# Two tiles of batches 0 and 1 through seven half-size products, the weights' differences earlier, and mask products on 120 of 128 columns

## The chip, the cores and the metric

The kernel runs on one core of one Trainium2 chip. The core has a matrix engine (PE; its weight loads are shown as PEld), a vector engine (DVE), an activation engine (ACT), a general engine (POOL), a queue engine for transfers (SP), and 16 DMA engines. Every engine works through its own list of instructions in order, and engines wait for each other by semaphores. The metric is the device time of one execution in microseconds; smaller is better.

## The reference, cut to what matters

```
q, k, v: (4 batches, 8 heads, 768 tokens, 64)
scores = (q @ k^T) / 8
mask   = same or neighbouring block of 32 tokens | first or last block, as row or as column
         | three sampled blocks per block row
attn   = softmax(where(mask, scores, -1e9));   x = attn @ v       -> (4, 768, 512)
a1     = alpha1 * x + beta1
u      = x + lam * (w_tok @ a1)                # over the 768 tokens
a2     = alpha2 * u + beta2
out    = u + lam * (relu(a2 @ w_ch1) @ w_ch2)  # 512 -> 2048 -> 512
```

The change concerns the last product, `relu(...) @ w_ch2` (768 x 2048 by 2048 x 512 in each batch), and the mask of the attention.

## The kernel before, in words

The 768 tokens of a batch are six tiles of 128 (`o` = 0 to 5): partition p of tile o holds token 6p + o. Two heads form a pair, so there are 16 pairs, four to a batch. The scores of a pair are made in nine units: an "A" unit is 2 x 128 keys by four query tiles (512 columns), a "B" unit holds the two remaining query tiles of two key pairs. A unit is `emit_qk` (PE, L600, into PSUM), `emit_exp` (ACT, L618, into the tile eT), from pair 5 on `emit_keep` (DVE, L635: eT times the 0/1 mask `mask01`, all 1024 numbers of a partition), and `emit_pv` or `emit_pv_keys` (PE, L647 or L670, weights times v, with a sum column). When a head is complete `emit_finish` divides (DVE, L687, L688) and `emit_a1pp` scales (two steps, L704 and L705, mostly on POOL).

The rest of a batch's work is cut into jobs: `job_tok2` (L844, the product over tokens; the addition L856 and two casts L863 on DVE), `emit_udma` (a transposing transfer, L894, issued by SP), `emit_uscale` (DVE, L885), `job_f1` (L910, the first channel product, 32 jobs in a batch; ACT writes the relu into `hts`, L917) and, for the second channel product, `job_f2` (L930): a quarter of a tile, four matmuls of 512 columns into one PSUM tile `mm`; the fourth quarter is followed by the addition into `x_sb` (DVE, L939) and the store (SP, L943). `mm` tiles rotate through three PSUM banks.

Batches 2 and 3 (`STR = (2, 3)`) already compute part of the second channel product in another way. Take tiles t and t+3 as two block rows, the hidden units as two halves, and the output columns as two halves (`lo`, `hi`). The eight half-size block products are replaced by seven:

```
weights, once:   T1 = B12 - B11   T2 = B22 - T1   T4 = B21 - T2   T3 = B22 - B12       job_t, DVE, L972
per two tiles:   X1 = A21 + A22   X2 = X1 - A11   A21 <- A11 - A21   A12 <- A12 - X2   job_s 1..4, DVE, L1018
products:        1: A11 B11   2: A12 B21   6: X2 T2   5: X1 T1                         job_p, PE, L1044
                 7: (A21) T3  4: A22 T4    3: (A12) B22
```

Each product is eight matmuls of 256 columns and is followed by an addition into `x_sb` (`plus`, DVE, L1054). Products 1, 6 and 5 accumulate in one PSUM bank, and 7 and 4 in another: the bank is read by the addition behind each of them before the next product is accumulated on top. The T blocks lie in buffers of the first phase that are free by then (`qTs`, `kTs`, `qk0`, `tmore`). In batch 2 these are tiles (1, 4) and (2, 5), in batch 3 all six.

What sets the order: the first 45 units (pairs 0 to 4) follow a plan with due times; all that comes after them follows the strings `W1`, `W2`, `W2L`, `W3`, one string for three units. A letter emits one thing: `q` the three units' score products and the first exponential, `x` an exponential, `k` a mask product, `p` a value product of one key pair, `f` a `job_f1`, `g` the next job of the second channel product, `T` a `job_tok2`, `d` an `emit_udma`, `v` an `emit_uscale`, `Y` a copy of v, `A` a `job_t` of two rows, `S` a `job_s`. On each engine the instructions run in this order. `g` takes its jobs from a list: 24 per batch where all six tiles go by `job_f2`. The strings are named here by their lines: W2 is L55 to L66, W2L L69 to L80. While W2 runs, batch 0's second channel product ends (strings L55 to L59); while W2L runs, batch 1's does (L69 to L73), with the same letters. By the first score product of each string the profile has them at these times: L45 at 63.55 us, L55 at 102.14, L56 at 105.62, L57 at 116.32, L58 at 120.14, L59 at 123.47; and in W2L, L70 at 174.16, L71 at 184.87, L72 at 188.69, L73 at 192.01.

## Time and profile before

| | |
|---|---|
| median of 3 runs | 300.72 us (300.29 to 301.11) |
| profiled execution | 300.64 us |
| its span, first to last instruction | 298.6 us |
| PE busy | 292.3 us (98%) |
| DVE busy | 219.5 us (74%) |
| ACT busy | 218.6 us (73%) |
| POOL busy | 109.7 us (37%) |

The span is 2.04 us shorter than the profiled execution's own time. The busy share of PE is a share of time in which at least one matmul is in flight; it is not a share of the peak.

### The profile page before, as it was taken

The numbers are of one execution on the slowest core, as the hardware profiler recorded it, in microseconds if no ns is written. First come the engines' busy times: TensorE is split into PE (matmuls) and PEld (weight loads), VectorE is DVE, ScalarE is ACT, GpSimd is POOL, SyncE is SP. The second block draws the span as 40 slices with busy tenths as digits, with TensorE's granted clock in tenths as the row PEclk, the third lists the DMA queues.
The fourth block names the chain that finished last, engine by engine and source line by source line (L and its number), as shares of the span: only waits on it lengthen the run. The fifth ranks groups of instructions, "written<-read, shape, count | busy, mean of one in ns | idle before, by whom it ended". The sixth has DMA issues, their size and how long they took to land.

```text
span 298.6 us, 7517 instructions
## 1 busy us (share of the span) xinstructions
PE 292.3 (98%) x3113; PEld 194.5 (65%) x3113; DVE 219.5 (74%) x434; ACT 218.6 (73%) x324; POOL 109.7 (37%) x149
## 2 busy tenths in 40 slices
PE   7999999999999999999999999999999999999995
PEld 3688888665567565565576465565566589666884
DVE  4988999995678797978778777892756889204674
ACT  4999999998799963999779581999869734677100
POOL 8997887632443710355323340344320300000000
PEclk9999999999999999999999999999999999999999
DMA  6999999971392992729844777727321112300032
GB/s 178 201 193 168 192 156 204 190 121 26 94 151 50 120 201 75 121 61 134 119 85 76 121 119 143 114 72 89 50 61 30 25 37 57 113 0 2 0 140 74
DMA packets 57273, 31.08 MB, mean 104 GB/s; under 512 B 37204, under 2 KB 54016, under 8 KB 57240
## 3 DMA queue, kind: packets, MB, share of 16 engines
q0 software_dynamic: 16752, 14.22, 33.2%
q1 hardware_dynamic: 40020, 15.92, 27.9%
q8 instruction: 24, 0.39, 0.6%
q10 hardware_dynamic: 468, 0.47, 0.5%
q14 instruction: 9, 0.07, 0.1%
HBM read 29.75 MB, written 6.29 MB: 121 GB/s over the span
## 4 chain that ended last, share of the span: by engine, by line
PE 83%; DVE 6%; DMA 6%; ACT 3%; POOL 1%; issue 1%; ACTq 0%; SPq 0%; POOLq 0%
PE mm L910 27%; PE mm L930 15%; PE sp L600 8%; PE mm L844 8%; PE op L670 7%; PE mm L1044 5%; PE sp L1044 4%; PE mm L600 3%; DMA qpad<-in_q_dram 3%; ACT eT L618 2%; PE op L647 2%; DVE eT L635 2%; PE mm L820 1%; DMA uraw<-ubf 1%; DMA ms<-ms_c 1%
## 5 line engine op out<-in xcount | busy, mean ns | idle before, releaser
L618 ACT ACTIVATE eT<-sp,expb 128x1024 f16<-128x1024 f32 x111 | 118.4, 1120 | 2.2 <-PE sp L600 1.6
L910 PE MATMUL mm<-uT,w1b 128*128 128x384 bf16 x512 | 91.6, 326 | 0.1
L635 DVE TENSOR_TENSOR eT<-eT,mask 128x1024 f16<-128x1024 f16 x99 | 80.3, 840 | 13.9 <-ACT eT L618 13.7
L917 ACT ACTIVATE hts<-mm 128x384 bf16<-128x384 f32 x128 | 60.9, 500 | 16.5 <-PE mm L910 15.9
L704 POOL TENSOR_TENSOR a1pp<-x_sb,vbc 128x384 bf16<-128x384 f32 x25 | 28.5, 1140 | 119.3 <-DVE x_sb L688 85.3
L910 PEld LDWEIGHTS <-w1b 128*128 128x128 bf16 x512 | 48.1, 98 | 32.0 <-issue 2.4
L618 ACT ACTIVATE eT<-mm,expb 128x512 f16<-128x512 f32 x66 | 41.7, 685 | 26.5 <-PE mm L600 26.2
L930 PE MATMUL mm<-w2b,hts 128*128 128x512 bf16 x224 | 54.7, 379 | 0.0
L670 PEld LDWEIGHTS <-eT 128*128 128x128 f16 x792 | 29.8, 98 | 8.7 <-issue 1.7
L930 PEld LDWEIGHTS <-hts 128*128 128x128 bf16 x224 | 19.8, 98 | 22.3 <-issue 3.9
L670 PE MATMUL op<-vext,eT 128*128 128x65 f16 x792 | 32.1, 194 | 0.1
L600 PE MATMUL sp<-qTs,kTs 88*128 88x512 bf16 (+1 forms) x120 | 26.9, 326 | 1.4 <-ACT eT L618 0.7
L705 POOL TENSOR_TENSOR a1pp<-a1pp,vbc 128x384 bf16<-128x384 bf16 x25 | 26.7, 1069 | 2.0
L844 PE MATMUL mm<-a1pp,wtokT 128*128 128x256 bf16 x216 | 25.9, 273 | 0.1
L844 PEld LDWEIGHTS <-wtokT 128*128 128x128 bf16 x216 | 20.6, 98 | 5.6 <-issue 1.8
L1044 PEld LDWEIGHTS <-hts 128*128 128x128 bf16 x208 | 19.6, 98 | 3.0 <-issue 0.3
L600 PE MATMUL sp<-qhT,khT 64*128 64x256 bf16 (+1 forms) x176 | 19.8, 322 | 0.0
L856 DVE TENSOR_TENSOR x_sb<-x_sb,mm 128x512 f32<-128x512 f32 x18 | 12.3, 685 | 9.9 <-PE mm L844 9.8
L600 PEld LDWEIGHTS <-khT 64*128 64x128 bf16 x264 | 10.6, 94 | 12.7 <-issue 9.2
L647 PEld LDWEIGHTS <-eT 128*128 128x128 f16 x360 | 14.9, 98 | 3.8 <-issue 0.3
L1018 DVE TENSOR_TENSOR xs<-hts 128x512 bf16<-128x512 bf16 (+1 forms) x8 | 3.7, 487 | 17.8 <-ACT hts L917 17.8
L688 DVE TENSOR_TENSOR x_sb<-op,rcp 128x384 f32<-128x384 f32 x28 | 15.6, 557 | 1.0
(117 smaller groups left out, 322.3 us busy)
## 6 DMA issues: line engine op xcount, KB each, us to landing
out_dram<-x_sb SPq DMA_DIRECT2D x23, 256.0 KB
qpad<-in_q_dram POOLq DMA_DIRECT2D x15, 192.0 KB, 4.6
kr<-in_k_dram POOLq DMA_DIRECT2D x15, 192.0 KB, 5.6
vr<-in_v_dram POOLq DMA_DIRECT2D x15, 192.0 KB, 6.2
w1b<-in_moe_w_ch_dram POOLq DMA_DIRECT2D x4, 512.0 KB, 9.3
w2b<-in_moe_w_ch_dram POOLq DMA_DIRECT2D x4, 512.0 KB, 8.4
hts<-in_moe_w_tok_dram POOLq DMA_DIRECT2D x2, 576.0 KB, 9.2
x_sb<-in_k_dram ACTq DMA_DIRECT2D x2, 192.0 KB
```

The lines of the kernel that those rows point to most:

```text
L600: nc.tensor.matmul(sp[jj][:, dst], lhsT, rhs, start=True, stop=True, skip_group_check=True,)
L618: nc.scalar.activation(dst, at, AF.Exp, bias=expb[:], scale=SCALE)
L635: nc.vector.tensor_mul(out=e, in0=e, in1=keep)
L647: nc.tensor.matmul(op[0][:, o, :], ets[u][:, jj, h * QB + n * P : h * QB + n * P + P], vexts[i % NVB][:, w, 2 * jp + jj, :], start=op[1] == 0,
L670: nc.tensor.matmul(op[0][:, o, :], ets[u][:, jj, h * QB + n * P : h * QB + n * P + P], vexts[i % NVB][:, w, 2 * jp + jj, :], start=op[1] == 0,
L704: eng.tensor_tensor(out=dst, in0=x_sbs[b][:, :, cols], in1=bc[0], op=ALU.mult)
L705: eng.tensor_tensor(out=dst, in0=dst, in1=bc[1], op=ALU.add)
L844: nc.tensor.matmul(ps[:, o], wtokT[:, os_, ts(2 * n + o, P)], a1pps[i][:, os_, :], start=(os_ == 0 and o == 0), stop=(os_ == NT - 1 and o ...
L910: nc.tensor.matmul(ps[:, 0:QC], w1b[:, dk, ts(n, P)], uTs[b][:, dk, ts(c, QC)], start=(dk == 0), stop=(dk == 3),)
L917: nc.scalar.activation(hts[(b, c)][:, n, :], ps[:, 0:QC], AF.Relu)
L930: nc.tensor.matmul(ps[:], ht[:, nk, ts(o % 3, P)], w2b[:, nk, :], start=(nk == 0), stop=(nk == NH - 1),)
L1044: nc.tensor.matmul(ps, a_of(b, t, a)[:, r], b_rows(m, r)[:, 0, cols], start=(start and r == 0), stop=(r == HN - 1), skip_group_check=True,)
```

## The change

Three things are edited.

First, batches 0 and 1 join `STR`. Their tiles 3 and 4 form one quad, which is put last in the list that `g` works through: tiles 0, 1, 2 and 5 go by `job_f2` (16 jobs), then products 2, 1, 6, 5, 7, 4, 3 of the quad. That is 23 jobs instead of 24, so one `g` per batch goes, and four `S` come in: one `g` of L56 (and L70) becomes an `S`, two `S` stand between products 1 and 6 in L57 (L71), and one stands at the end of L58 (L72). Products 1 of batches 0 and 1 use an `mm` bank. The code names the two tiles of a quad by a pair instead of t and t+3.

Second, the sixteen `A` (the differences of the weights) move from W2 (strings L60, L61, L64) to the strings L45, L47, L48, L49, L51, L52 of W1 and L55 of W2.

Third, the mask product of an "A" unit leaves out the first four and last four of each 128 query columns. By the assertion these are tokens of the first or last block, whose rows of the mask are all ones. It covers 128 x (8 x 120) numbers instead of 128 x 1024. "B" units are unchanged.

```diff
-    "q Y 0 f 1 k p 2 x f f f x f k k p f g",
+    "q Y 0 f 1 k A A A p 2 x f f f x f k k p f g",
...
-    "q Q 0 g x g f v v s T T x k 1 k p p g g T g g Y d 2 k",
-    "q g 0 k g d 1 2 p x k g x k",
-    "q 0 p k x v Q v 1 2 p k x g k g",
+    "q Q 0 g x g f v v s T T x k 1 k p p g g T g S Y d 2 k",
+    "q g 0 k S S g d 1 2 p x k g x k",
+    "q 0 p k x v Q v 1 2 p k x g k g S",
     "q 0 p 1 g x k f K k x f p p k 2 f",
-    "q k 0 f x f p s f f x 1 L p k 2 f f f k Y A A A A A f",
-    "q f L f 0 f k A A A A A A A A 1 f Y x f p g x f p f g k k 2",
+    "q k 0 f x f p s f f x 1 L p k 2 f f f k Y f",
+    "q f L f 0 f k 1 f Y x f p g x f p f g k k 2",
...
-STR = (2, 3)
+STR = (0, 1, 2, 3)
...
+    KQ = slice(BLK // NT - 1, P - BLK // NT + 1)
+    for p in list(range(KQ.start)) + list(range(KQ.stop, P)):
+        assert {(NT * p + o) // BLK for o in range(NT)} <= {0, NBLK - 1}
...
-            keep, e = mask01[:, 2 * jp : 2 * jp + 2, 0:QA], eT[:]
+            keep, e = (
+                t.rearrange("p j (m q) -> p j m q", q=P)[:, :, :, KQ]
+                for t in (mask01[:, 2 * jp : 2 * jp + 2, 0:QA], eT[:])
+            )
...
     P_ORDER = {
+        0: direct(0, 1, 2, 5) + quad((3, 4), (2, 1, 6, 5, 7, 4, 3)),
+        1: direct(0, 1, 2, 5) + quad((3, 4), (2, 1, 6, 5, 7, 4, 3)),
...
     S_ORDER = {
+        0: [((3, 4), n, ALL) for n in (1, 2, 3, 4)],
+        1: [((3, 4), n, ALL) for n in (1, 2, 3, 4)],
```

## The prediction

> **What bounds the kernel.** I read the page first, then the chain that ended last, then the stretches where the edits lie, engine by engine.

> ```profile
> PE 292.3 (98%) x3113; PEld 194.5 (65%) x3113; DVE 219.5 (74%) x434; ACT 218.6 (73%) x324; POOL 109.7 (37%) x149
> PE 83%; DVE 6%; DMA 6%; ACT 3%; POOL 1%; issue 1%; ACTq 0%; SPq 0%; POOLq 0%
> ...
> 183.21 1.73 PE mm L930 x8
> ...
> 276.59 0.87 PE sp L1044 x8
> ```

> PE is in flight for 98% of the span and makes 83% of the chain. In the two rows of the chain, eight matmuls of 512 columns take 1.73 (0.216 each) and eight of 256 columns 0.87 (0.109 each). So a shorter list for PE would shorten the run, and any wait put into PE's list lengthens it, if no idle time was there before. Whether DVE can serve in time is asked of the stretches of the strings (columns: stretch, its length, busy time of the engines):

> ```profile
> 63.55:105.62 42.07, 42.07 (x446) 25.30 (x446) 31.16 (x55) 37.55 (x57) 18.27 (x20) 1.00 0.61 83
> 116.32:120.14 3.82, 3.82 (x33) 1.77 (x33) 2.25 (x5) 3.28 (x4) 0.00 (x0) 1.00 0.26 52
> 120.14:123.47 3.33, 3.33 (x43) 1.75 (x42) 3.33 (x4) 2.91 (x4) 2.55 (x2) 1.00 0.80 196
> 123.47:128.24 4.77, 4.77 (x61) 2.97 (x60) 4.74 (x10) 4.52 (x7) 1.67 (x2) 1.00 0.70 82
> 134.90:142.90 8.00, 8.00 (x70) 4.48 (x68) 6.84 (x20) 6.85 (x13) 4.03 (x6) 1.00 1.11 143
> ```

> PE fills every stretch. In L58 and L59 (rows three and four) DVE is full as well: 3.33 of 3.33 and 4.74 of 4.77. There, and in L57, the change puts its DVE steps.

> **What PE saves.** Two tiles by `job_f2` are 32 matmuls of 512 columns, 32 x 0.216 = 6.92; a quad is 56 of 256, 56 x 0.109 = 6.10. That is 0.82 per batch, 1.64 in all, since each product (0.87) takes the place of a quarter tile (0.865) and one quarter goes. This is on the path.

> **What DVE gets.** Per quad four half sums and seven additions, in place of two additions of 512.

> ```profile
> L1018 DVE TENSOR_TENSOR hts<-hts,xs 128x1024 bf16<-128x1024 bf16 x5 | 3.4, 684 | 0.0
> L1018 DVE TENSOR_TENSOR xs<-xs,hts 128x512 bf16<-128x512 bf16 x6 | 2.4, 422 | 0.1
> L1054 DVE TENSOR_TENSOR x_sb<-x_sb,mm 128x256 f32<-128x256 f32 x15 | 6.2, 416 | 2.3 <-PE mm L1044 2.3
> L1054 DVE TENSOR_TENSOR x_sb<-x_sb,sp 128x512 f32<-128x512 f32 x5 | 3.4, 682 | 0.9 <-PE sp L1044 0.9
> L635 DVE TENSOR_TENSOR eT<-eT,mask x99: 676/684/1494, 59.1 to 239.8; 128x1024 f16<-128x1024 f16 x99
> L972 DVE TENSOR_TENSOR kTs<-w2b,qTs x4: 418/420/420, 137.8 to 138.8; 128x512 bf16<-128x512 bf16 x4
> ```

> 4 x 0.684 + 6 x 0.416 + 0.682 - 2 x 0.68 = 4.6 per quad. What matters more is where these steps stand, so I walk the strings L56 to L59 with the times of before, PE first, then DVE and POOL:

> ```profile
> 114.50 1.89 PE L930 MATMUL mm<-w2b,hts 128*128 128x512 bf16 x8
> 116.32 0.39 PE L600 MATMUL mm<-qhT,khT 64*128 64x256 bf16 x4
> ...
> 117.08 1.90 PE L930 MATMUL mm<-w2b,hts 128*128 128x512 bf16 x8
> 118.82 0.53 PE L670 MATMUL op<-vext,eT 128*128 128x65 f16 x12
> 119.18 1.03 PE L930 MATMUL mm<-w2b,hts 128*128 128x512 bf16 x4
> 120.14 0.39 PE L600 MATMUL mm<-qhT,khT 64*128 64x512 bf16 x2
> ...
> 120.90 0.91 PE L670 MATMUL op<-vext,eT 128*128 128x65 f16 x24
> 121.64 1.89 PE L930 MATMUL mm<-w2b,hts 128*128 128x512 bf16 x8
> 123.47 0.39 PE L600 MATMUL mm<-qhT,khT 64*128 64x512 bf16 x2
> ...
> 124.60 1.03 PE L930 MATMUL mm<-w2b,hts 128*128 128x512 bf16 x4
> 125.46 1.46 PE L910 MATMUL mm<-uT,w1b 128*128 128x384 bf16 x8
> ```

> ```profile
> 115.84 0.36 DVE L328 COPY vext<-vr 128x768 f16<-128x768 f16 x1
> 116.11 0.69 DVE L635 TENSOR_TENSOR eT<-eT,mask 128x1024 f16<-128x1024 f16 x1
> 118.05 0.69 DVE L635 TENSOR_TENSOR eT<-eT,mask 128x1024 f16<-128x1024 f16 x1 [1.26 <-ACT eT L618]
> 119.02 0.69 DVE L939 TENSOR_TENSOR x_sb<-x_sb,mm 128x512 f32<-128x512 f32 x1 [0.28 <-PE mm L930]
> 119.62 0.19 DVE L687 RECIPROCAL rcp<-op 128x6 f32<-128x6 f32 x1
> 119.84 0.56 DVE L688 TENSOR_TENSOR x_sb<-op,rcp 128x384 f32<-128x384 f32 x1
> 120.32 3.42 DVE L635 TENSOR_TENSOR eT<-eT,mask 128x1024 f16<-128x1024 f16 x3
> 123.66 0.86 DVE L885 TENSOR_SCALAR uT<-uraw,ab2T 128x768 bf16<-128x768 bf16 x2
> 124.44 1.28 DVE L635 TENSOR_TENSOR eT<-eT,mask 128x1024 f16<-128x1024 f16 x2
> ```

> ```profile
> 120.56 1.30 POOL L704 TENSOR_TENSOR a1pp<-x_sb,vbc 128x384 bf16<-128x384 f32 x1 [15.20 <-PE mm L600]
> 121.94 1.25 POOL L705 TENSOR_TENSOR a1pp<-a1pp,vbc 128x384 bf16<-128x384 bf16 x1
> ```

> How the walk counts: on DVE a successor starts 0.08 before the recorded end (two mask products of 0.68 take 1.28), so a half sum costs 0.60, a 256-column addition 0.34, the 512-column one 0.60. DVE starts 0.04 after PE's last matmul (117.08 + 1.90 = 118.98, addition at 119.02), and I take 0.05 the other way. An "A" mask product of 960 numbers: 0.422 + 448 x (0.684 - 0.422)/512 = 0.65, so 0.57.

> *L57, the wait for X2.* Product 2 runs 114.50 to 115.37, so L57's scores begin at 115.46 (0.86 earlier than before: the saving) and end at 116.22. Product 1 needs a free bank (addition 2 on DVE, 115.84 to 116.26) and runs 116.30 to 117.17. Behind it in PE's list stands product 6, which reads X2. DVE's list is addition 2, S1 (116.18), copy of v, mask product (117.06), addition 1 (117.63), mask product (117.97; its exponential came 1.73 behind the scores before, 116.32 to 118.05, so it is ready at about 117.19), S2 (118.57 to 119.26), S3. So product 6 starts at 119.30: PE waits 2.1 with scores, exponentials and value products queued behind it. It ends at 120.17, the value product at 120.53. Product 5 goes on in the bank that addition 6 reads (120.37 to 120.79): it starts at 120.84, waiting 0.3, and ends at 121.71. L58 thus starts at 121.71 in place of 120.14.

> *L58, the wait between 7 and 4.* Scores to 122.47, two value products to 123.21, product 7 to 124.08. Product 4 accumulates in 7's bank, with no PE work between, and must wait for addition 7. DVE before that: reciprocal and division (120.71 to 121.49), mask product (121.41), addition 5 (121.98), mask product (122.58), mask product, two L885 steps of 0.39, mask product, addition 7. POOL's two steps start 0.16 behind the division, at 121.65, and last until 124.28. Of the three mask products at 120.32 the trace gives 3.42 in place of 1.89 (three times 0.60, and 0.08) while POOL ran; the longest of L635 is 1.494. I take 1.22 for the one at 122.58 and 0.90 for the next, which POOL covers only by half. Then L885 at 124.70, a mask product at 125.48, addition 7 from 126.08 to 126.50, product 4 at 126.55: a wait of 2.5. It ends at 127.42. The ends: 1.8 with no slowing by POOL (the exponentials, 1.7 behind the scores, then hold the mask product until 123.4), and 0.5 if DVE had nothing in its list but the addition. I take 2.5, as the POOL steps are released by the division in the same place as before.

> [...]

> *L59.* Scores from 127.42 to 128.18, value product to 128.54. Addition 4 at 127.62, S4 127.96 to 128.65; product 3 reads S4's result: 128.70 to 129.57. Before, the work behind it started at 125.46. So PE comes out of the four strings 129.57 - 125.46 = 4.1 later: 5.2 of waits less 1.0 of work saved, counting 0.2 of small gaps behind value products that go.

> **Batch 1.** L70 to L73 hold the same letters as L56 to L59, and the profile has them 68.55 later with the same distances (184.87, 188.69, 192.01 against 116.32, 120.14, 123.47). One thing differs:

> ```profile
> 193.12 0.48 DVE L885 TENSOR_SCALAR uT<-uraw,ab2T 128x768 bf16<-128x768 bf16 x1 [0.45 <-DMA uraw<-ubf]
> ...
> 195.55 0.79 PEld L670 LDWEIGHTS <-eT 128*128 128x128 f16 x24 [0.46 <-DVE x_sb L688]
> ```

> Before, SP issued the second `uraw` transfer behind the store of tile 4, and DVE waited 0.45 for it; PE lost about 0.25 in the end. In the new order that store comes later, so both `uraw` transfers go one behind the other and this loss goes: 4.1 - 0.25 = 3.85. For batch 0 the move on SP gives nothing (L885 did not wait at 123.66); the stores that move back have no reader.

> **The sixteen differences** cost 16 x 0.34 = 5.4 of DVE between 63.55 and 105.62, where DVE has 42.07 - 31.16 = 10.9 idle. I cost them at 0; with the cover gone, the mask product behind three of them is 1.0 late and PE waits for it; the upper end is 5.4, and I keep 1 for the range. Where they are taken away (134.90 to 142.90) PE was full, so that gives 0.

> **The shorter mask products** save 66 x 0.03 = 2 on DVE. Outside the walk PE is full, so 0 there; the form (8 x 120) is not in the trace. Its nearest row is the half sum over 8 pieces of 128 at 684, so I take 651; the far end is 1494.

> **Sum.** 300.64 (the profiled execution; 298.6 of span and 2.04 around it) + 4.1 + 3.85 = 308.6. The median of the runs, 300.72, is 0.08 off, which is nothing here; 0.3% (0.9) is about what a measurement of this kernel can tell from no change.

> **The rivals.** *No wait lasts (faster).* If DVE were 2.1 ahead in L57, X2 would be ready at 117.2, and 2.5 ahead in L58 for addition 7, PE would keep its saving: 300.64 - 2 x 0.82 = 299.0. It decides at waits of 1.0 per batch. For it: 1.26 of idle time at 118.05. Against: that idle time is already used up by S1 and S2 in the walk, and the two full strings. 6%, of which 1 for waits so near 1.0 that nothing can be measured.
> *Only X2 is waited for.* If DVE's list is shorter than I think in L58, the wait there falls to 0.5 and each batch loses 2.1: 300.64 + 2.1 + 1.9 = 304.6. Against it is DVE's 3.33 of 3.33. 7%.
> *The 120-column form loses speed.* At 1.49 each, two per string cost 1.6 where a string has some 1.2 idle (10.9 over nine): 33 x 0.4 more, 322. Against: the row of the half sum. 3%.
> *The clock falls.* The rows of the opening show matmuls at a lower rate:

> ```profile
> L480 PE MATMUL op<-const-bfloat16-1.0 128*128 128x512 bf16 x12 | 5.0, 564 | 0.8 <-PEq L1379 0.8
> ```

> Twelve took 5.0 where 12 x 0.216 = 2.6 would do. If each of the four waits above 2 brought such a loss of 2.4, the time would be 318. [...] 2%.
> *The differences are not covered* or more strings are disturbed, above 311: 4%.

> **The numbers.** My own case has 78%, 307.2 (1.8 in place of 2.5, twice) to 310.2. The range takes in the case of X2 alone in part and the cover that may be gone: 304.6 to 311.0. Faster 0.05, same 0.01, slower 0.94.

> **What would show it.** In the waits: PE or PEld of the products' line idle behind DVE, about 2 in L57 and 2.5 in L58, and the same in L71 and L72; PE busy falls by some 1.6 while the span grows by 8; first matmul of the first channel product in L59 at about 129.6. It would be wrong if PE shows no wait at product 6, if the mask products of 960 numbers are not near 651, or if waits turn up between 63.55 and 105.62.

## The result and the profile after

The changed kernel takes 308.28 us in the median of four runs (307.90 to 308.74), the kernel before 300.62 beside it (300.29 to 301.11): 1.0254 times the time, 95% interval 1.0232 to 1.0277. Its profiled execution took 308.0 us, with a span of 306.3.

In the new numbering the lines of the prediction's steps are: mask product L641 (was L635), value product L676, scores L603, products L1048, half sums L1025, additions L1058, first channel product L916, scaling of u L891, POOL's scaling L710 and L711. The busy times and the clock row of the page of the changed kernel (40 equal slices of the span, the granted clock in tenths):

```profile
PE 292.2 (95%) x3146; PEld 199.9 (65%) x3161; DVE 223.2 (73%) x452; ACT 218.7 (71%) x324; POOL 109.0 (36%) x149
...
PEclk9999999999999999999999999799999999999999
```

PE is as busy as before, over a span 7.7 longer. The PEclk row has a 7, of which more below. First the waits in the products' line (idle time in all, how often, the longest), then PE's list in batch 0 from L57 to L59 in order of time (start, length, engine, line, operation, count, idle time before it and what ended that):

```profile
PEld L1048 <- DVE xs L1025: 4.5, 2, 2.2
...
PE mm L1048 <- DVE xs L1025: 3.9, 2, 1.9
PE mm L1048 <- DVE x_sb L1058: 3.3, 2, 2.2
```

```profile
115.78 1.03 PE L1048 MATMUL mm<-w2b,hts 128*128 128x256 bf16 x8
118.76 0.61 PE L1048 MATMUL mm<-qTs,xs 128*128 128x256 bf16 x4 [1.95 <-DVE xs L1025]
...
120.32 1.03 PE L1048 MATMUL mm<-qTs,xs 128*128 128x256 bf16 x8
121.29 0.39 PE L603 MATMUL mm<-qhT,khT 64*128 64x512 bf16 x2
...
122.79 0.82 PE L1048 MATMUL mm<-qk,hts 128*128 128x256 bf16 x6
...
125.99 1.03 PE L1048 MATMUL mm<-kTs,hts 128*128 128x256 bf16 x8 [2.16 <-DVE x_sb L1058]
126.96 0.39 PE L603 MATMUL mm<-qhT,khT 64*128 64x512 bf16 x2
...
128.14 1.05 PE L1048 MATMUL mm<-w2b,hts 128*128 128x256 bf16 x8
129.03 1.46 PE L916 MATMUL mm<-uT,w1b 128*128 128x384 bf16 x8
```

The two waits stand where the walk had them, at product 6 (for X2) and between products 7 and 4. DVE's and POOL's lists of the same stretch show who is late:

```profile
115.64 0.68 DVE L1025 TENSOR_TENSOR xs<-hts 128x1024 bf16<-128x1024 bf16 x1
...
118.02 0.69 DVE L1025 TENSOR_TENSOR xs<-xs,hts 128x1024 bf16<-128x1024 bf16 x1
...
120.92 0.65 DVE L641 TENSOR_TENSOR eT<-eT,mask 128x960 f16<-128x960 f16 x1
121.48 0.68 DVE L1058 TENSOR_TENSOR x_sb<-x_sb,mm 128x512 f32<-128x512 f32 x1
122.08 2.15 DVE L641 TENSOR_TENSOR eT<-eT,mask 128x960 f16<-128x960 f16 x2
124.15 0.86 DVE L891 TENSOR_SCALAR uT<-uraw,ab2T 128x768 bf16<-128x768 bf16 x2
...
125.53 0.41 DVE L1058 TENSOR_TENSOR x_sb<-x_sb,mm 128x256 f32<-128x256 f32 x1
```

```profile
121.16 1.26 POOL L710 TENSOR_TENSOR a1pp<-x_sb,vbc 128x384 bf16<-128x384 f32 x1 [16.36 <-DVE x_sb L694]
122.50 1.21 POOL L711 TENSOR_TENSOR a1pp<-a1pp,vbc 128x384 bf16<-128x384 bf16 x1
```

X2 ends at 118.71 and product 6 starts at 118.76; addition 7 ends at 125.94 and product 4 starts at 125.99.

Batch 1 has the same 1.95 before product 6, and then something that the kernel before does not show:

```profile
192.95 1.86 PE L1048 MATMUL mm<-qTs,xs 128*128 128x256 bf16 x8
...
195.15 1.06 PE L603 MATMUL sp<-qhT,khT 64*128 64x256 bf16 x6
...
199.11 1.03 PE L1048 MATMUL mm<-kTs,hts 128*128 128x256 bf16 x8 [1.11 <-DVE x_sb L1058]
```

Product 5 took 1.86 here and 1.03 in batch 0. Two stretches of 3.41 us, and what PE did in them (columns: stretch, its length, busy time and instructions of PE, PEld, DVE, ACT, POOL, the granted clock, the DMA share, GB/s):

```profile
189.52:192.93 3.41, 1.41 (x20) 1.23 (x21) 2.87 (x7) 1.77 (x2) 0.00 (x0) 1.00 1.01 128
192.93:196.34 3.41, 3.39 (x20) 1.63 (x20) 2.72 (x5) 0.95 (x2) 2.18 (x2) 0.50 0.45 89
```

The clock stood at half for 3.41 us, behind a stretch of the same length in which PE was busy for 1.41. DVE went on, so part of the lost time came off the next wait, which fell from 2.16 to 1.11.

### The profile page after: what moved, and what is told of

It is laid out like the page before. It is cut to its first block, busy times and chain, and to the rows that moved or that the text cites. A ratio compares the mean times of both kernels' runs of the same rounds, so it can differ in the third digit from the quotient of the medians.

```text
span 306.3 us, 7617 instructions
## 1 busy us (share of the span) xinstructions
PE 292.2 (95%) x3146; PEld 199.9 (65%) x3161; DVE 223.2 (73%) x452; ACT 218.7 (71%) x324; POOL 109.0 (36%) x149
## 4 chain that ended last, share of the span: by engine, by line
PE 90%; DVE 5%; ACT 2%; issue 1%; DMA 1%; ACTq 0%
PE mm L916 27%; PE mm L936 11%; PE sp L603 10%; PE mm L1048 9%; PE mm L850 8%; PE op L676 8%; PE sp L1048 4%; PE mm L603 3%; PE mm L826 3%; PE op L653 2%; DVE eT L641 2%; PE mm L653 1%; ACT eT L621 1%; DVE x_sb L1058 1%; DMA ms<-ms_c 1%
## 5 line engine op out<-in xcount | busy, mean ns | idle before, releaser
L916 PE MATMUL mm<-uT,w1b 128*128 128x384 bf16 x512 | 91.6, 326 | 0.0
L641 DVE TENSOR_TENSOR eT<-eT,mask 128x960 f16<-128x960 f16 (+1 forms) x99 | 76.5, 794 | 14.3 <-ACT eT L621 13.8
L710 POOL TENSOR_TENSOR a1pp<-x_sb,vbc 128x384 bf16<-128x384 f32 x25 | 28.3, 1132 | 127.9 <-DVE x_sb L694 122.7
L916 PEld LDWEIGHTS <-w1b 128*128 128x128 bf16 x512 | 48.1, 98 | 31.5 <-issue 2.3
L936 PE MATMUL mm<-w2b,hts 128*128 128x512 bf16 x145 | 37.2, 380 | 0.7 <-issue 0.2
L676 PEld LDWEIGHTS <-eT 128*128 128x128 f16 x792 | 29.9, 98 | 8.3 <-issue 2.0
L1048 PEld LDWEIGHTS <-hts 128*128 128x128 bf16 x288 | 27.0, 98 | 8.2 <-issue 4.8
L676 PE MATMUL op<-vext,eT 128*128 128x65 f16 x792 | 32.2, 194 | 0.2
L603 PE MATMUL sp<-qTs,kTs 88*128 88x512 bf16 (+1 forms) x120 | 26.9, 325 | 1.3 <-ACT eT L621 0.7
L711 POOL TENSOR_TENSOR a1pp<-a1pp,vbc 128x384 bf16<-128x384 bf16 x25 | 26.1, 1043 | 2.0
L936 PEld LDWEIGHTS <-hts 128*128 128x128 bf16 x160 | 14.1, 98 | 16.3 <-issue 3.1
L603 PE MATMUL sp<-qhT,khT 64*128 64x256 bf16 (+1 forms) x176 | 20.3, 329 | 0.0
L1058 DVE TENSOR_TENSOR x_sb<-x_sb,mm 128x256 f32<-128x256 f32 (+2 forms) x32 | 14.2, 447 | 6.1 <-PE mm L1048 5.6
L603 PEld LDWEIGHTS <-khT 64*128 64x128 bf16 x264 | 10.5, 95 | 11.8 <-issue 8.4
L1025 DVE TENSOR_TENSOR xs<-hts 128x512 bf16<-128x512 bf16 (+1 forms) x10 | 5.1, 526 | 17.8 <-ACT hts L923 17.8
```

The costliest lines, as they stand in the source:

```text
L603: nc.tensor.matmul(sp[jj][:, dst], lhsT, rhs, start=True, stop=True, skip_group_check=True,)
L641: nc.vector.tensor_mul(out=e, in0=e, in1=keep)
L676: nc.tensor.matmul(op[0][:, o, :], ets[u][:, jj, h * QB + n * P : h * QB + n * P + P], vexts[i % NVB][:, w, 2 * jp + jj, :], start=op[1] == 0,
L710: eng.tensor_tensor(out=dst, in0=x_sbs[b][:, :, cols], in1=bc[0], op=ALU.mult)
L711: eng.tensor_tensor(out=dst, in0=dst, in1=bc[1], op=ALU.add)
L916: nc.tensor.matmul(ps[:, 0:QC], w1b[:, dk, ts(n, P)], uTs[b][:, dk, ts(c, QC)], start=(dk == 0), stop=(dk == 3),)
```

## The experiments

The lag of a string is its start in a run's profile less its start in the profile before: the changed kernel's is -0.53 at L56, -1.37 at L57, +3.57 at L60 and +7.89 at L74. The -0.53 is older than any edited instruction (it is -0.49 at the string of 57.3 us already, ahead of the first mask product). At L56 the profiles of these runs differ by up to 1.9 from each other, so the steps below are differences of two lags of one profile.

**Everything but the quads.** Batches 0 and 1 leave the list of quads; the early differences and the shorter mask products stay. (Here and below, edits of W2's strings are made in W2L too, where nothing else is said.)

```diff
-    "q Q 0 g x g f v v s T T x k 1 k p p g g T g S Y d 2 k",
-    "q g 0 k S S g d 1 2 p x k g x k",
-    "q 0 p k x v Q v 1 2 p k x g k g S",
+    "q Q 0 g x g f v v s T T x k 1 k p p g g T g g Y d 2 k",
+    "q g 0 k g d 1 2 p x k g x k",
+    "q 0 p k x v Q v 1 2 p k x g k g",
...
-STR = (0, 1, 2, 3)
+STR = (2, 3)
```

> The differences of the weights moved to W1 and the shorter mask products, without the quads of batches 0 and 1 (six tiles by job_f2 again, letters of before in L56 to L58 and L70 to L72). Theory (the time is lost by waits of PE inside the two quads): within 0.9 of before, 300.6, since DVE has 10.9 us idle for the 5.4 us of differences and PE is full elsewhere. Rival (the sixteen differences in W1 push mask products back, or the 960-number form is slow): 303 or more, with waits of PE for L641 between 63 and 106 us.

Measured: 299.80 (299.45 to 300.14), before 300.40; ratio 0.9977 [0.9967, 0.9987]. So the whole loss is the quads', and the rest gains 0.6, more than the 0 of the prediction; what that gain is made of is asked at the end of this section.

**A quad in batch 0 alone.** `STR = (0, 2, 3)`, and W2L's strings as before.

> The changed kernel with the quad in batch 0 alone; batch 1 goes by job_f2 with the letters of before. Theory: each quad costs its own waits, batch 0's PE comes out 4.1 us later, so 304.7, and the clock stays at 1.000 because the fall was seen in batch 1's quad alone. Rival (the loss comes from the fall of the clock, seen once at about 193 us): near 301. Rival (the loss is in the parts shared by both, differences and masks): 307 or more.

Measured: 305.17 (303.44 to 305.70), ratio 1.0145 [1.0112, 1.0179]. One quad costs somewhat more than half of two. Against the expectation the clock did not stay at 1.00: three of four runs had it at 0.994, which is one such stretch in the profiled one, and took 304.77 to 305.70; the run without took 303.44. The profiled run shows the fall behind X2's wait in batch 0, where the changed kernel's profile had none (the same columns as above):

```profile
115.91:119.32 3.41, 1.46 (x13) 1.03 (x12) 3.41 (x8) 3.01 (x4) 0.00 (x0) 1.00 0.59 115
119.32:122.73 3.41, 3.41 (x27) 2.53 (x25) 1.99 (x5) 0.00 (x0) 0.41 (x1) 0.50 0.60 125
```

**Every product in its own bank.** Products 6, 5 and 4 of batches 0 and 1 do not accumulate on another's bank (so the two tiles lack the terms that were accumulated); DVE's list is the same.

```diff
+        own = b < B - 2
+        if own and n in (4, 5, 6):
+            bk[7 if n == 4 else 1] = mm_tile()[:]
...
-            mul(b, t, 4, bk[7][:, lo], False)
+            mul(b, t, 4, bk[7][:, lo], own)
```

> In the quads of batches 0 and 1 products 6, 5 and 4 go to a PSUM bank of their own instead of accumulating on 1, 6 and 7, so they do not wait for the addition that reads the bank; all additions stay, so the output tiles 3 and 4 of these batches lack the terms that were accumulated. Theory A (DVE's list sets the pace, the bank is only where PE meets it): the wait between 7 and 4 goes, but product 3 then waits for S4, which DVE reaches at about the same time as before: 0.6 us less per batch, 307.2. Theory B (the shared bank itself costs the 2.2 and 0.3 us): 2.5 us less per batch, 303.5.

Measured: 308.56 (307.45 to 310.04), ratio 1.0285 [1.0253, 1.0317]: not B, and by its waits A, though above A's 307.2; the mean clock was 0.987 to 0.994 in all four runs. Batch 1 of the profile had no half clock, and there PE went from L71's scores to the first channel product in 13.43 us, against 14.08 in the changed kernel's batch 0: 0.65 less. The wait only moved behind product 4, to L73's scores, which need a bank that addition 7 has to read, and to product 3 (PE's list, batch 1):

```profile
196.58 1.04 PE L1048 MATMUL mm<-kTs,hts 128*128 128x256 bf16 x8
...
199.22 0.37 PE L603 MATMUL mm<-qhT,khT 64*128 64x512 bf16 x1 [1.29 <-DVE x_sb L1058]
...
200.73 1.05 PE L1048 MATMUL mm<-w2b,hts 128*128 128x256 bf16 x8 [0.22 <-DVE hts L1025]
```

So DVE's list sets the pace, whichever instruction of PE meets it first.

**No half sums.** In batches 0 and 1 the products read the halves of `hts` in place of X1, X2 and the sums (so two tiles of these batches come out with other numbers); the four half sums go from DVE.

```diff
+        if b < B - 2:
+            a, need = {"X1": "21", "X2": "22"}.get(a, a), 0
...
-        0: [((3, 4), n, ALL) for n in (1, 2, 3, 4)],
-        1: [((3, 4), n, ALL) for n in (1, 2, 3, 4)],
+        0: [],
+        1: [],
```

> The four half sums of the quads of batches 0 and 1 are left out; products 6, 5, 7 and 3 read the unsummed halves of hts instead, so the output tiles 3 and 4 of these batches are not the reference's. Theory A: the wait of 2 us for X2 shrinks to some 0.7 (addition 1 behind product 1), the wait between 7 and 4 stays near 2.3 because DVE still has its mask products and L885 ahead of addition 7; 2.4 us lost per batch in place of 4.1: 305.2. Theory C (only the half sums cost, their 4 x 0.6 us of DVE): the quads would cost nothing or gain, 300 to 301.

Measured: 306.06 (304.34 to 307.92), ratio 1.0186 [1.0126, 1.0246]: 304.34 and 304.51 where the clock held, 307.6 and 307.9 where it fell. In the profile, without a fall, PE comes out of the strings 2.58 later in each batch, 0.25 of it given back in batch 1. X2's wait becomes one of 0.51 for a bank, and the other stays (PE's list of this run in batch 0):

```profile
117.20 0.60 PE L1050 MATMUL mm<-qTs,hts 128*128 128x256 bf16 x4 [0.51 <-DVE x_sb L1060]
...
124.42 1.03 PE L1050 MATMUL mm<-kTs,hts 128*128 128x256 bf16 x8 [2.17 <-DVE x_sb L1060]
```

So the half sums cost 1.5 per batch, and the additions with their place in DVE's list more than that.

**X2 earlier.** Half sums 1 to 3 go into L56 (L70); the casts and the scaling of u there go to ACT.

```diff
-    "q Q 0 g x g f v v s T T x k 1 k p p g g T g S Y d 2 k",
-    "q g 0 k S S g d 1 2 p x k g x k",
+    "q Q 0 g x g f v v s S T S T S x k 1 k p p g g T g Y d 2 k",
+    "q g 0 k g d 1 2 p x k g x k",
...
-        copy = nc.scalar.copy if i >= NPAIR - 2 else nc.vector.tensor_copy
+        act = i >= NPAIR - 2 or phase.get("act")
+        copy = nc.scalar.copy if act else nc.vector.tensor_copy
...
```

> The changed kernel, with half sums 1 to 3 in L56 (L70), ahead of L57's scores, and the two casts and the scaling of u in that string on ACT, which is idle there for 7 us, to give DVE room. If X2 is late only because of its place in DVE's list, the wait of 1.95 at product 6 falls to what the bank costs (about 0.65: product 1 or 6 behind an addition), the wait of 2.16 between 7 and 4 stays near 2.4, PE comes out of L59 2.5 later than before instead of 4.1, and the time is 300.4 + 2 x 2.5 - 0.25 = 305.2 (304.5 if the 0.6 of the opening is gained here too). If the half sums in L56 push DVE's other steps there out by their own 1.9, the wait moves to the first product of L57 and nothing is gained: 308.

Measured: 307.93 (305.68 to 309.39), ratio 1.0250 [1.0215, 1.0285]. In batch 0 the parts are as expected (PE's list):

```profile
116.96 0.60 PE L1049 MATMUL mm<-qTs,xs 128*128 128x256 bf16 x4 [0.51 <-DVE x_sb L1059]
...
124.18 1.03 PE L1049 MATMUL mm<-kTs,hts 128*128 128x256 bf16 x8 [2.17 <-DVE x_sb L1059]
```

PE comes out 2.59 later (expected 2.5). The total missed by 2.7, for the clock: batch 1 of the same profile lost 3.82 with the same waits and one half-clock stretch (mean clock 0.994), and the other three runs had 0.989, the mean of two such stretches. In that batch the wait of 2.16 behind product 7 lay whole in one stretch of 3.41 us (191.95 to 195.36, PE busy for 1.25 of it), and the next was at 0.50: here this wait is all the idle time of the stretch ahead of the fall.

**POOL's steps put off, first try.** The two scaling steps behind the division of L57 (L71) are emitted at L60 (L74).

```diff
+        elif i in (2 * NP, 3 * NP):
+            todo["P"].append(lambda: emit_a1pp(i, w, nc.gpsimd))
...
-    "q k 0 f x f p s f f x 1 L p k 2 f f f k Y f",
+    "q P P k 0 f x f p s f f x 1 L p k 2 f f f k Y f",
```

> The changed kernel, with POOL's two scaling steps behind the division of L57 (and L71) put off to the start of L60 (L74), so that no POOL step runs beside L58's mask products. In the changed kernel two mask products there took 2.15 together where 1.22 would do. If POOL slows them and they set the wait between products 7 and 4, that wait falls from 2.16 to about 1.5 (then the exponential, 1.7 behind L58's scores, holds the first of them), and the time is 308.3 - 2 x 0.6 = 307.1. If the mask products are held by something else, their 2.15 and the wait stay as they are: 308.3. If what is put off comes back at L60, the wait falls but PE loses the same there: 308.3 too, and the rows at L60 show it.

Measured: 309.71 (309.01 to 310.68), ratio 1.0308 [1.0287, 1.0330]. The edit did nothing: nothing else stands in POOL's list between the two places, so every engine's list is the changed kernel's, and POOL starts the step as soon as the division is done. The run tells nothing of POOL, but it is a second measurement of the changed kernel, 1.4 above the first. Its profile says where one part of that is from, a transfer that came late at 39 us, ahead of all edits (a row of PE's list; the changed kernel's first profile has no wait there):

```profile
39.02 0.51 PE L510 MATMUL mm<-ident,kr 128*128 128x128 bf16 x6 [1.32 <-DMA kr<-in_k_dram]
```

The rest is the clock: it fell in batch 0, which cost 5.62, and held in batch 1, which cost 6.72 to 10.55, 3.83.

**POOL's steps held back.** Now a copy on POOL ahead of these steps reads the scaled u of L58 (L72), so that they run behind the two mask products.

```diff
+        elif t == "H":
+            nc.gpsimd.tensor_copy(out=held[:], in_=phase["u"])
...
-    "q 0 p k x v Q v 1 2 p k x g k g S",
+    "q 0 p k x v Q v H P 1 2 p k x g k g S",
...
```

> The changed kernel with POOL's two scaling steps of L57 (L71) held back by a copy on POOL that reads the scaled u of L58 (L72), so that they run behind L58's two mask products (2.15 in the changed kernel) and not beside them. If POOL slows these and they set the wait between 7 and 4, they take 1.25 to 1.55, the wait falls from 2.16 to about 1.6, and the time is 308.3 - 1.1 = 307.2; what the steps slow behind them (mask product, half sum 4) may give back up to 0.5 per batch. If the slowness has another cause, 2.15 and 2.16 stay.

Measured: 308.71 (307.13 to 309.74), ratio 1.0280 [1.0249, 1.0311]. DVE's and POOL's lists in batch 0:

```profile
123.53 0.65 DVE L641 TENSOR_TENSOR eT<-eT,mask 128x960 f16<-128x960 f16 x1
124.54 0.66 DVE L641 TENSOR_TENSOR eT<-eT,mask 128x960 f16<-128x960 f16 x1 [0.36 <-ACT eT L621]
...
126.82 1.27 DVE L641 TENSOR_TENSOR eT<-eT,mask 128x960 f16<-128x960 f16 x1
...
128.37 1.04 DVE L1026 TENSOR_TENSOR hts<-hts,xs 128x1024 bf16<-128x1024 bf16 x1
```

```profile
126.59 0.99 POOL L710 TENSOR_TENSOR a1pp<-x_sb,vbc 128x384 bf16<-128x384 f32 x1
127.66 1.21 POOL L711 TENSOR_TENSOR a1pp<-a1pp,vbc 128x384 bf16<-128x384 bf16 x1
```

Without POOL beside them the two mask products take 0.65 and 0.66, not 2.15 together, and the slowness goes with POOL to the mask product at 126.82 (1.27) and half sum 4 (1.04). In batch 1 the same two take 0.65 and 0.66, and behind them 1.27 (at 200.27) and 1.04 (at 201.82). So the slowness goes where POOL's steps go. The hold is worth little here: the wait at product 4 is 1.61 in place of 2.16, and from the end of L58's scores to the end of addition 7 batch 0 takes 3.34 instead of 3.90, since the exponential then holds the second mask product, and 0.24 comes back at product 3, which waits for half sum 4. In the total nothing is left; the clock fell in both batches of this profile.

**Another order.** With X2 early, value products and scores stand between products that share a bank, and addition 7 ahead of the scaling of u. (The edit of the first try on POOL is in it too, and does nothing.)

```diff
-    "q g 0 k S S g d 1 2 p x k g x k",
-    "q 0 p k x v Q v 1 2 p k x g k g S",
+    "q g 0 k p g d 1 2 x k S x",
+    "q g 0 p p k x k g v Q v 1 2 x k g k",
```

> Both edits (POOL's steps put off; half sums 1 to 3 in L56 and ACT in DVE's place) and another order in L57 and L58 (L71 and L72): value products and the scores of the next string stand between products that share a bank, and addition 7 stands ahead of the scaling of u. If the waits are what costs the 8 us, and nothing of the quad itself, PE comes out of L59 within 1 us of before and keeps at most its 0.8 per batch: 299.5 to 301.5. If DVE's eleven added steps are too much for these strings in any order, waits of 2 or more per batch stay in other places: 304 or more.

Measured: 302.61 (302.45 to 303.15), ratio 1.0083 [1.0069, 1.0096], between the two expectations. X2's wait is gone, and one of 1.8 between 7 and 4 is left in each batch (PE's list, batch 0):

```profile
123.44 1.03 PE L1049 MATMUL mm<-kTs,hts 128*128 128x256 bf16 x8 [1.79 <-DVE x_sb L1059]
```

**All waits of the products covered.** On top of the order above (with POOL's steps as in the changed kernel), product 4 goes behind L59's scores and a value product, addition 7 ahead of the mask products.

```diff
-    "q g 0 k p g d 1 2 x k S x",
-    "q g 0 p p k x k g v Q v 1 2 x k g k",
-    "q 0 p 1 g x k f K k x f p p k 2 f",
+    "q g 0 k p g d 1 2 x k x",
+    "q g 0 p p S k g x k v Q v 1 2 x k k",
+    "q p g 0 1 g x k f K k x f p p k 2 f",
```

> The run with the reordered strings still had one wait, 1.8 between products 7 and 4 in each batch. Here product 4 goes behind L59's scores and a value product (L73 in batch 1), and addition 7 ahead of the mask products; half sum 4 goes behind addition 5. POOL's steps are where the changed kernel has them. If waits are all that the quad costs, PE comes out of L59 0.3 earlier than before in each batch, and the time is 299 to 300 (with the shorter masks' 0.4 in it); if a quad cannot be had for nothing here (banks, exponentials or the exchange of smaller matmuls cost what it saves), 301 or more.

Measured: 300.36 (299.98 to 302.24), ratio 1.0011 [0.9997, 1.0025]. Eight microseconds are gone with no work taken out, but the quad's saving is not had either: PE comes out of L59 0.44 later than before. Of that PE's list shows, in batch 0:

```profile
116.69 0.53 PE L676 MATMUL op<-vext,eT 128*128 128x65 f16 x12
117.36 0.60 PE L1049 MATMUL mm<-qTs,xs 128*128 128x256 bf16 x4
...
122.82 0.39 PE L603 MATMUL sp<-qhT,khT 64*128 64x512 bf16 x2 [0.36 <-ACT eT L621]
```

a wait of 0.36 for an exponential, and 0.67 from the start of a value product to that of product 6, where 0.37 is usual (addition 1 frees the bank only at 117.31). They make up 0.66 of the 1.28 that the strings lose (the saving of 0.84 and the 0.44); the rest is in smaller gaps and isn't accounted for one by one.

**The value product ahead of L59's scores.** The diff is against the run before.

```diff
-    "q g 0 p p S k g x k v Q v 1 2 x k k",
-    "q p g 0 1 g x k f K k x f p p k 2 f",
+    "q g 0 p p S k g p x k v Q v 1 2 x k k",
+    "q g 0 1 g x k f K k x f p p k 2 f",
```

> The run with all waits of the products covered left PE 0.36 of a wait for an exponential at L59's last score unit, and came out of L59 0.44 later than before, relative to L56. Here the value product of L59 stands ahead of L59's scores, so that the exponential has 0.4 more. If that wait is what keeps the saving, PE comes out of L59 about as in the kernel before or 0.2 earlier, and the time is 299.3 to 299.8, the same as or less than with the shorter masks alone. If POOL's second pair of steps, which this moves 1.5 earlier, slows the mask products in L59 in turn, the wait moves there and the time stays at 300.4.

Measured: 304.15 (303.69 to 304.84), ratio 1.0131 [1.0109, 1.0153]: worse than either expectation. The division now comes earlier, and POOL's second pair of steps with it, onto the scaling of u. POOL's, DVE's and PE's list in batch 0:

```profile
123.71 1.34 POOL L710 TENSOR_TENSOR a1pp<-x_sb,vbc 128x384 bf16<-128x384 f32 x1 [2.67 <-DVE x_sb L694]
125.13 0.92 POOL L711 TENSOR_TENSOR a1pp<-a1pp,vbc 128x384 bf16<-128x384 bf16 x1
```

```profile
123.55 0.65 DVE L641 TENSOR_TENSOR eT<-eT,mask 128x960 f16<-128x960 f16 x1
124.12 2.15 DVE L892 TENSOR_SCALAR uT<-uraw,ab2T 128x768 bf16<-128x768 bf16 x2
```

```profile
126.32 0.32 PE L917 MATMUL mm<-uT,w1b 128*128 128x384 bf16 x1 [0.42 <-DVE uT L892]
127.82 0.81 PE L917 MATMUL mm<-uT,w1b 128*128 128x384 bf16 x4 [1.18 <-DVE x_sb L1059]
```

Two steps that took 0.86 behind POOL's (124.15 in the changed kernel) took 2.15 beside them, the additions behind came late, and PE waited for u and for a bank. The rows look like those of L58, on an instruction that was not thought of; no run holds POOL back here, so that POOL is the cause is not shown for it.

**The shorter mask products alone**, twice.

```diff
-            keep, e = mask01[:, 2 * jp : 2 * jp + 2, 0:QA], eT[:]
+            keep, e = (
+                t.rearrange("p j (m q) -> p j m q", q=P)[:, :, :, KQ]
+                for t in (mask01[:, 2 * jp : 2 * jp + 2, 0:QA], eT[:])
+            )
```

> The kernel before, with the shorter mask products alone. By the prediction this is worth nothing, as PE is full: 300.4, within 0.3% of before. If the 0.6 that the run without quads gained comes from the mask products (less time, or less traffic to SBUF), this run shows it: 299.8.

> The kernel before with the shorter mask products alone, a second time, beside the run above on the same chip. If its 0.4 below before was no chance, it is 0.2 to 0.6 below before again; by the prediction's 0 it is within 0.2.

Measured: 299.79 (299.26 to 300.44) against 300.16, ratio 0.9986 [0.9978, 0.9995], and 299.62 (299.13 to 300.02) against 300.04, ratio 0.9979 [0.9967, 0.9991]. The edit is worth 0.4 both times, and with it alone the kernel beats both kernels of this case. But next to nothing of the 0.4 lies between the first and the last instruction: the medians of the span are 298.1 against 298.1 and 297.9 against 297.95. What differs is the time outside the span: 1.66 to 1.76 in each of these 24 runs, 1.99 to 2.11 in each of the 33 beside them. The run without quads has 1.72 there against 2.04, half of its 0.6. So within the span the shorter mask products gain less than 0.1; why the time outside it falls by 0.3 no run shows.

## Why the prediction was right

The direction, the size (308.6 against 308.28) and the place were right, and in batch 0 so was each step. That the totals come within 0.3 is in part luck. The profiled execution (308.0) had four things that the sum has not: 0.53 gained in the opening, 0.2 behind L74, 0.3 outside the span (1.7 in place of 2.04), and 0.5 lost by one fall of the clock. A second measurement of the same lists gave 309.71. The mechanism is told by the steps. The walk's times less the 0.53 by which this profile is ahead at L56, against the rows above:

| step, batch 0 | walk | less 0.53 | measured |
|---|---|---|---|
| product 6 (X2 ready) | 119.30 | 118.77 | 118.76 |
| product 5 | 120.84 | 120.31 | 120.32 |
| L58's scores | 121.71 | 121.18 | 121.29 |
| product 4 (addition 7 done) | 126.55 | 126.02 | 125.99 |
| L59's scores | 127.42 | 126.89 | 126.96 |
| product 3 (half sum 4 done) | 128.70 | 128.17 | 128.14 |
| first channel product | 129.57 | 129.04 | 129.03 |

- *The saving* of 0.82 per batch: 0.84 at L57 (-0.53 to -1.37).
- *The waits*: 1.95 for 2.1 and 2.16 for 2.5. The starts behind them hit; the work before ended later, as a product's row ends 1.03 behind its start and the walk took 0.87, and product 7 began 0.11 late.
- *Batch 1*, 3.85: the second run of the same lists has 3.83 there with a full clock, and the waits of batch 0 again. In the first profile it was 4.32, the half clock's work. The scaling of u no longer waits for the transfer in either, as the 0.25 says.
- *The sixteen differences*, 0: right. PE took 42.06 for L45 to L55 as before, while DVE did 71 instructions in place of 55 (the stretch from L45 to L56 in the changed kernel):

```profile
63.03:105.09 42.06, 41.85 (x441) 25.30 (x445) 36.50 (x71) 37.54 (x57) 18.15 (x20) 1.00 0.62 85
```

- *The masks' form*: 0.65 where POOL is away (123.53 in the run that holds it back), as taken. *Their worth*, 0, held within the span. The measured 0.4 lies outside it, in the 2.04 that the sum took over unchanged.
- *POOL*: the two mask products held DVE for 2.07 (122.08 to 124.15) against the walk's 1.22 + 0.90 = 2.12, and the hold shows the cause. The sum hit and its parts did not: one by one they took 0.86 and 1.22, the longer one second. The mask product at 120.92 began 0.24 ahead of POOL and took 0.65, so it was not stretched; POOL's step took longer there, 1.26 for the 0.99 of the run that holds it back (126.59), where it began 0.23 ahead of a mask product and that one took 1.27. In these two pairs the one that began first kept its length; what holds for other steps no run was made to show. The 310.2 at the end of the forecast's own case takes 0.8 more per batch at this mask product; no run shows that term, and 0.65 stands in its place.
- *PE's busy time* was to fall by 1.6 and did not (292.2). The matmuls at half clock took longer: 0.83 at product 5 and 0.68 at the scores behind it (1.06 and 0.61 for 0.60 and 0.39) make up 1.5 of it.
- *The step that failed* is the clock's: a fall in the quads was given 2%, a chance that no run stood behind. In three of the four runs of the first measurement and all four of the second the mean clock shows one such fall or two (0.993 to 0.994, or 0.989). It did not decide, because a fall cost 0.5 to 1.5 and not 2.4: 0.5 in the first profile's batch 1 (4.32 for 3.83), 1.5 in batch 0 of the second (5.62 for 4.10), where it came behind the second wait and hid nothing.

Of the rivals, "X2 alone" and "no wait lasts" are both refuted by the waits; with the waits taken away by another order the second gave 300.4 and not 299.0.

## What to carry to other kernels

When work goes from PE to an engine that is full in the same stretch, write that engine's list down by the letters and see when each result is ready: here the starts came out within 0.1 us, and the total of saved matmul time said nothing. Between two products of a shared bank, put other PE work that lasts as long as what stands ahead of the addition in DVE's list. Before a step is moved, ask which helper engine it releases earlier and which list that engine then disturbs. And before a small gain is put down to an edited step, compare the spans: here 0.3 of 0.4 lay outside them.

## What the runs showed that was not expected

```profile
118.73:122.14 3.41, 1.61 (x22) 1.42 (x23) 2.83 (x8) 1.54 (x2) 0.00 (x0) 1.00 0.67 138
122.14:125.56 3.42, 3.31 (x48) 2.34 (x47) 3.36 (x5) 2.23 (x4) 2.48 (x2) 1.00 0.34 66
125.56:128.97 3.41, 1.35 (x14) 0.94 (x15) 2.85 (x7) 1.04 (x2) 0.00 (x0) 1.00 0.00 0
128.97:132.39 3.42, 3.42 (x29) 2.10 (x25) 1.66 (x5) 2.38 (x3) 0.99 (x1) 0.50 0.21 77
```

So a wait of 2 us halved the clock or not, by how the stretches cut it. In the changed kernel X2's wait of 1.95 lay in one stretch in batch 1 (189.52 to 192.93) all but for 0.07; in batch 0 it was shared by two, with 2.38 and 2.34 of PE in flight (114.42 to 121.25), and the wait between 7 and 4 by the next two, with 2.58 and 2.09, and the clock stayed at 1.00. This and a late transfer (below) set the two profiles of the same lists apart, 308.00 and 310.68.

**The opening is not the same in every run.** A transfer of `kr` or `qpad` at 37 to 41 us cost PE 1.32 in the profile of the second run of the changed kernel's lists, 0.24 in that of the kernel before, and nothing in the first run's and that of the shorter masks. In the first 7 us PE waited 0.65 for `kTs` in the kernel before, 0.55 in the changed one and 0.3 with the quad in batch 0 alone. A difference of 0.5 between two profiles says nothing by itself.
